# Grouping the P times V matmuls and respacing the weight blocks of a fused attention and two-mixture kernel

## The chip, the cores and the metric

The kernel runs on one core of a Trainium2 chip. The metric is the device time of one execution in microseconds (us), as the median of several runs. The core has five engines with queues of their own: TensorE (PE; its weight loads are shown as PEld), VectorE (DVE), ScalarE (ACT), GpSimd (POOL) and SyncE (SP), which issues nearly all transfers.

## The reference

Attention for 4 batches x 8 heads, 576 positions, head size 64, with a causal mask and a decay bias from a running sum of s; the heads side by side (512 channels) go through a first mixture with a convolution gate, and that through a second mixture.

```python
scores = scale * q @ k.T                       # per head, 576 x 576
bias = -(cum[:, None] - cum[None, :])          # cum = cumsum(max(s, 0))
scores = where(causal, -1e9, scores + minimum(bias, 0))
attn = softmax(scores); out = attn @ v         # "P times V"
x = heads side by side                         # 4 x 576 x 512
h = maximum(x @ w_in, 0)                       # 512 -> 1024
gate = sigmoid(conv3(h, conv_w))
x = (h * gate) @ w_out                         # 1024 -> 512
u = x + (x.T @ U @ V).T
out = u + maximum(u @ w_ch1, 0) @ w_ch2        # 512 -> 2048 -> 512
```

The weights of the mixtures are 64-bit floats and lie in memory as pairs of 32-bit words.

## The kernel before

**A planner sets the order.** Every piece of work is entered with `plan.op(engine, cost, function, reads, writes)`. `Plan.order()` then walks through a model of time: each engine takes, of the entries whose inputs are ready by the model, the one that was entered first. The program that results has one fixed order on each engine; on the chip each instruction waits for its semaphores in that order. The entries' costs shape the order and do nothing else. PSUM banks (8) are handed out by the same walk, with a limit for each class (`CAPS`).

**Attention.** `att_head(h)` enters the work of head h: the transfers for the next head (`prep4` for heads 0 to 7; `prep` and `place` later), the score tiles (`scores`, `scores4`; the products in line 675 and 691, tile sc), maxima on VectorE (line 636), exponentials on ScalarE (line 653, tile P, p for the last 64 rows), the division by the row sum on GpSimd (line 664). For the head before, `transp` turns P's 128 x 128 blocks on PE (line 798, tile pt) in four groups, each of which ScalarE copies to th (line 352). Heads 0 to 7 (`FS`) take q and k in full precision (tile qkF); later heads split them into two parts (tiles t, placed into qkA and qkB).

**P times V.** `av(h, half)` serves a pair of heads. The first half (query positions 0 to 255) needs group 0 of both heads, the second (256 to 575, 320 columns) groups 1, 2 and 3. Each key block j of a group is one entry before the change: two in the first half, five in the second, of 320, 320, 320, 192 and 64 columns. All entries of a half add into one accumulator ps, so they run in their order; the third entry of the second half is the first that needs group 3. An entry holds two matmuls, one for each head of the pair: their 64 columns of V go to columns 0 and 64 of the array (`tile_position`), their outputs to partitions 0 and 64. The profile shows each as two instructions (line 824, tile av). A copy to x follows (line 837), then x's split into xh and xl, on which `m1_in` works.

**First mixture.** `m1_in` multiplies x by the weight blocks w1h and w1l (line 868, tile h) and `m1_out` the gated result by the blocks w1o (line 910, tile y). The parts of batch b are entered among the heads of batch b + 1; PE takes them when attention has nothing ready. They are entered from head 9 on, the first `m1_out` at head 11.

**Weight blocks.** `w1_jobs` are 16 blocks: eight of the first product, then eight of the second. After `att_head(h)`, the loop at the end of the kernel enters each block n with `W1_AT[n] == h`. `load_split` makes a transfer of 512 KB into one of two raw buffers (SP, line 524), a scaling on ScalarE (line 501), three integer operations on VectorE (line 504 once, line 514 twice, tile wf_w), a cast on ScalarE (line 352) and a subtraction on GpSimd (line 364). `load_cw` brings the convolution's 24 columns in the same way at head `CW_AT`. SP issues its transfers in the planned order, and one that waits for a raw buffer holds up those behind it.

**Second mixture.** Behind attention come the splits of u and the weights, the products ma_S and ma_A (line 1153) and the products my (line 1252).

Of the kernel before, what the change touches and what calls it, by code (L numbers as in the profile page):

```python
# [35 lines left out]

WI, WO, WP, WM = 0.3, 1.5, 0.3, 0.2

W1_AT = [0, 1, 1, 2, 3, 4, 5, 5, 6, 7, 7, 8, 9, 10, 10, 11]
CW_AT = 9  # L40
MIX_AT = 12

AHEAD = 80
# [8 lines left out]
def f32(ap):  # L52
    return ap.bitcast(F32)
# [255 lines left out]
def tile_attention_moe_mixer(  # L309
# [21 lines left out]
    def act(n, fn, r, w, extra=0):  # L331
        return plan.op("ACT", (157 if st.get("late") else 53) + n * 0.834 + extra, fn, r, w)

    def pool(n, fn, r, w, two=False, extra=125):
        return plan.op("POOL", ((280 if st.get("late") else 148) + n * 2.1) if two else (37 + n * 0.834 + extra), fn, r, w)
# [8 lines left out]
    def pe(ns, fn, r, w):  # L344
        return plan.op("PE", ns, fn, r, w)
# [5 lines left out]
    def hi_act(out, src, r, w, n):  # L351
        act(n, lambda: nc.scalar.copy(out(), src()), r, w)  # L352
# [10 lines left out]
    def lo_pool(out, src, hi, r, w, n):  # L363
        pool(n, lambda: nc.gpsimd.tensor_tensor(out(), src(), f32(hi()), ALU.subtract), r, w, two=True)  # L364


    st = {}
# [12 lines left out]
    def ring(pool_, cls, count, shape, dtype, name, at={}):  # L380
        n = at[pool_, cls] = at.get((pool_, cls), -1) + 1
        return pool_.buf(f"{cls}{n % count}", shape, dtype, name)

    def bank(cls, name):
        b = Buf(banks, None, [128, 512], F32, name, [banks.opened])
        b.cls = cls
        banks.live.append(b)
        plan.banked.append(b)
        return b
# [93 lines left out]
    for t in p4s:  # L483
        o = pool(64, lambda t=t: nc.gpsimd.memset(t[:, S:640], 0.0), [], [(t, "pad")], extra=0)
# [36 lines left out]
    def load_split(src, h, l, c, n, name):  # L521

        raw = ring(dec, "raw", RINGS["w64"], [128, 512], I64, f"raw_{name}")
        load = dma(n * 1024, lambda: nc.sync.dma_start(out=raw[:, :n], in_=src[:, c : c + n]), [], [raw])
        load.preds.add(st["first"])
        wf = ring(dec, "wf", RINGS["wf"], [128, 512], F32, f"wf_{name}")
        decode64(lambda: wf[:, :n], [wf], raw, n)
        hi_act(lambda: h[:, :n], lambda: wf[:, :n], [wf], [h], n)
        lo_pool(lambda: l[:, :n], lambda: wf[:, :n], lambda: h[:, :n], [wf, h], [l], n)

    def load_cw():
        raw = ring(dec, "raw", RINGS["w64"], [128, 512], I64, "raw_cw")
        dma(24576, lambda: nc.sync.dma_start(out=raw[:, :24], in_=cwU[:, :24]), [], [raw])
        decode64(cw, [cw], raw, 24)
        pool(24, lambda: nc.gpsimd.tensor_scalar(cw(), cw(), 2.0**-8, 1.0, ALU.mult, ALU.mult), [cw], [cw])
# [271 lines left out]
    def av(h, half):  # L807

        b, dt = h // H, h % H // 2
        n, q0, g0 = (256, 0, 0) if half == 0 else (320, 256, 2)  # L810
        vr = st["v", h // 2]
        ps = bank("av", f"av{h}_{half}")
        ops = []
        for g in [0] if half == 0 else [1, 2, 3]:
            for j, i0, i1 in GROUPS[g]:
                ops.append((i0 != g0, g, j, 128 * i0 - q0))
        ops.sort()
        for c, (_, g, j, o) in enumerate(ops):
            w = n - o
            pairs = [st[h + e][f"g{g}"] for e in range(2)]  # L820

            def mms(c=c, j=j, o=o, w=w, pairs=pairs):
                for e, (t, pos) in enumerate(pairs):
                    nc.tensor.matmul(
                        ps[64 * e : 64 * e + 64, o:n],
                        lhsT=vr[:, e, j, :],
                        rhs=t[:, pos[j] : pos[j] + w],
                        start=c == 0,
                        stop=c == len(ops) - 1,
                        tile_position=(0, 64 * e),  # L830
                    )

            pe(max(4 * w / 2.4, 160), mms, [vr, *(t for t, _ in pairs)], [ps])
        if half == 0:
            st["x", b, dt] = ring(ap, "x", RINGS["x"], [128, S], F32, f"x{b}_{dt}")
        x = st["x", b, dt]
        act(n, lambda: nc.scalar.copy(x[:, q0 : q0 + n], ps[:, :n]), [ps], [(x, half)])
        if half == 1:
            th = ring(xp, "xh", RINGS["xs"], [128, S + 2], F32R, f"xh{b}_{dt}")
            tl = ring(xp, "xl", RINGS["xs"], [128, S + 2], F32R, f"xl{b}_{dt}")  # L840
            for t in (th, tl):
                plan.op(
                    "POOL",
                    60,
                    lambda t=t: nc.gpsimd.memset(f32(t[:, 0 : S + 2 : S + 1]), 0.0),
                    [],
                    [(t, "pad")],
                )
            hi_act(lambda: th[:, 1 : S + 1], x, [x], [(th, "x")], S)
            lo_pool(lambda: tl[:, 1 : S + 1], x, lambda: th[:, 1 : S + 1], [x, (th, "x")], [(tl, "x")], S)  # L850
            xs[b, dt] = (th, tl)
# [441 lines left out]
    for c, n in ((0, 384), (512, 224)):  # L1293
        o = pool(n, lambda c=c, n=n: nc.gpsimd.memset(mask[:, c : c + n], 0.0), [], [(mask, c)], extra=0)
# [15 lines left out]
    def att_head(h):  # L1310
# [21 lines left out]
        if h > 0:  # L1332
            transp(h - 1, 1)
            if h % 2 == 0:
                av(h - 2, 0)
# [7 lines left out]
        if h > 0 and h % 2 == 0:  # L1343
            av(h - 2, 1)
# [28 lines left out]
    for h in range(NH + 1):  # L1373
# [11 lines left out]
        for n, (f, c) in enumerate(w1_jobs):  # L1385
            if h == W1_AT[n]:
                load_split(w1[f], w1h[f, c], w1l[f, c], c, 512, f"w1_{f}_{c}")
        if h == CW_AT:
            load_cw()
# [88 lines left out]
    for g in range(2):  # L1478
        blk = (w2a, u1p)[g].buf(f"u{g}", [128, 2 * 7 * S], F32R, f"w2_{g}")
        for i in range(7):  # L1480
            f = 7 * g + i
# [89 lines left out]
```

## Time and profile before

| | us |
|---|---|
| median of 3 runs (lowest to highest) | 837.72 (836.69 to 840.6) |
| the profiled execution | 835.59 |
| span of the profiled execution | 833.8 |
| PE busy in the span | 797.2 |
| DVE busy | 544.3 |
| ACT busy | 453.4 |
| POOL busy | 361.7 |

The profile is one execution; its span runs from the first to the last instruction. Times in a row are from the span's start. Matmuls overlap in PE's pipeline and their drawn lengths hold part of that overlap, so the distance between two starts says more than a length, and PE at full busy share isn't PE at its peak. Lines give the place in the kernel's text, and out<-in the tiles.

### The profile page before, as it was taken

Reading aid. Unit: us, or ns where it says so; the run is one execution under the profiler, and the core shown is the slowest. Engines: PE = TensorE matmul, PEld = TensorE weight load, DVE = VectorE, ACT = ScalarE, POOL = GpSimd, SP = SyncE. Lnnn points to the kernel's source line nnn. Section 1 sums busy time; section 2 is a strip of 40 time slices with the busy share of each in tenths; the row PEclk is TensorE's granted clock in tenths of the full one; section 3 lists DMA queues with packets and bytes.
Section 4 is the critical chain, followed back from the end, with each engine's and each line's share of the span. In section 5 each row is a group of like instructions: output and inputs, shape, how many; then the busy total and the mean of one; then the engine's idle time right before and its main releaser. Section 6 shows DMA issues by size and latency. Waiting matters only on the chain. (4 is left out here: it accounts for less than half of the span.)

```text
span 833.8 us, 15389 instructions
## 1 busy us (share of the span) xinstructions
PE 797.2 (96%) x5300; PEld 706.9 (85%) x5300; DVE 544.3 (65%) x1182; ACT 453.4 (54%) x1144; POOL 361.7 (43%) x441
## 2 busy tenths in 40 slices
PE   4989899999999999999998999999999999999998
PEld 2556687999889998989988998999998888888888
DVE  6878987635855377556898989777689632323232
ACT  4888887758868488676666334334344322222212
POOL 3768574543436344383275866455574200000000
PEclk9999999999999999999999999999999999999999
DMA  7656765644456256030225445546378563635443
GB/s 211 184 156 188 187 162 133 153 112 103 145 132 151 66 121 196 17 108 1 83 84 190 142 132 184 168 143 196 120 220 292 154 199 101 182 108 179 116 127 98
DMA packets 66310, 119.70 MB, mean 144 GB/s; under 512 B 9396, under 2 KB 34868, under 8 KB 66232
## 3 DMA queue, kind: packets, MB, share of 16 engines
q1 hardware_dynamic: 66160, 118.70, 49.1%
q8 instruction: 42, 0.69, 0.4%
q14 instruction: 36, 0.29, 0.1%
q10 hardware_dynamic: 72, 0.01, 0.0%
HBM read 68.81 MB, written 28.90 MB: 117 GB/s over the span
## 5 line engine op out<-in xcount | busy, mean ns | idle before, releaser
L1252 PE MATMUL my<-mh,w 128*128 128x512 f32 (+1 forms) x560 | 158.8, 368 | 0.0
L1153 PE MATMUL ma_S<-u,W 128*128 128x288 f32 x768 | 119.8, 296 | 5.6 <-DVE s L1169 5.5
L1233 DVE SCALAR_TENSOR_TENSOR ml<-ml,mh 128x512 fp32r<-128x512 f32 (+1 forms) x80 | 53.2, 672 | 107.9 <-ACT mh L1230 107.9
L1252 PEld LDWEIGHTS my<-mh,w 128*128 128x128 f32 x560 | 101.6, 189 | 17.5
L1230 ACT ACTIVATE mh<-ml 128x512 fp32r<-128x512 f32 (+1 forms) x80 | 46.8, 589 | 127.9 <-DMA ml<-ch_d 65.8
L1153 PEld LDWEIGHTS ma_S<-u,W 128*128 128x128 f32 x768 | 107.5, 188 | 7.9 <-DVE s L1169 7.9
L664 POOL TENSOR_SCALAR P<-P,sm 128x128 f32<-128x128 f32 (+3 forms) x128 | 75.9, 610 | 86.0 <-DVE sm L727 74.8
L910 PE MATMUL y<-gh,w1o 128*128 128x288 f32 x512 | 112.8, 299 | 0.0
L1252 PE MATMUL my<-ml,w 128*128 128x512 f32 (+1 forms) x280 | 103.0, 368 | 0.0
L636 DVE CUSTOM_DVE_ANT_0 sc<-sc,mask 128x128 f32<-128x128 f32 (+2 forms) x144 | 69.0, 497 | 46.5 <-PE sc L675 37.5
L1153 PE MATMUL ma_A<-u,W 128*128 128x288 f32 x576 | 92.5, 295 | 0.9 <-ACT p L1165 0.9
L364 POOL TENSOR_TENSOR gl<-c,gh 128x288 fp32r<-128x288 f32 x64 | 53.9, 850 | 74.9 <-ACT gh L895 66.8
L910 PEld LDWEIGHTS y<-gh,w1o 128*128 128x128 f32 x512 | 84.9, 188 | 1.5 <-issue 1.0
L868 PE MATMUL h<-xh,w1h 128*128 128x290 f32 x256 | 80.5, 315 | 3.4 <-ACT P L653 1.2
L1153 PEld LDWEIGHTS ma_A<-u,W 128*128 128x128 f32 x576 | 82.0, 188 | 1.6 <-ACT p L1165 1.1
L880 DVE SCALAR_TENSOR_TENSOR c<-h,cw,c 128x288 f32<-128x288 f32 x128 | 64.2, 512 | 24.2 <-ACT c L876 23.4
L868 PE MATMUL h<-xl,w1h 128*128 128x290 f32 x256 | 76.8, 300 | 0.7 <-POOL xl L364 0.7
L868 PE MATMUL h<-xh,w1l 128*128 128x290 f32 x256 | 76.7, 299 | 0.0
L653 ACT ACTIVATE P<-sc,sm 128x128 f32<-128x128 f32 (+3 forms) x128 | 68.2, 537 | 13.0 <-DVE sm L636 10.2
L910 PE MATMUL y<-gl,w1o 128*128 128x288 f32 x256 | 75.1, 293 | 0.0
L352 ACT COPY th<-pt 128x384 f32<-128x384 f32 (+2 forms) x128 | 63.4, 496 | 11.1 <-PE pt L798 9.5
L798 PE MATMUL pt<-ident,P 128*128 128x128 f32 x320 | 60.4, 276 | 1.5 <-POOL P L664 1.5
(139 smaller groups left out, 1748.2 us busy)
## 6 DMA issues: line engine op xcount, KB each, us to landing
ml<-ch_d SPq DMA_DIRECT2D x64, 256.0 KB, 2.8
ch_d<-p SPq DMA_DIRECT2D x64, 144.0 KB, 1.8
raw_w<-w_in SPq DMA_DIRECT2D x16, 512.0 KB, 3.2
raw_w2a<-w_in SPq DMA_DIRECT2D x16, 512.0 KB, 5.3
raw_w2b<-w_in SPq DMA_DIRECT2D x16, 512.0 KB, 4.7
t<-qk_in SPq DMA_DIRECT2D x24, 288.0 KB, 3.0
qkB<-t SPq DMA_DIRECT2D x24, 288.0 KB, 3.7
qkA<-t SPq DMA_DIRECT2D x24, 288.0 KB, 3.9
```

What stands on the lines that cost most here:

```text
L352: act(n, lambda: nc.scalar.copy(out(), src()), r, w)
L364: pool(n, lambda: nc.gpsimd.tensor_tensor(out(), src(), f32(hi()), ALU.subtract), r, w, two=True)
L636: lambda: nc.vector.tensor_tensor_reduce(out=ps[:rows, :w], in0=ps[:rows, :w], in1=mask[:rows, m0 : m0 + w], scale=-0.125, scalar=3.0e38 i ...
L653: lambda: nc.scalar.activation(out(), ps[:rows, :w], ACTF.Exp, bias=low(), scale=-1.0, accum_out=total()),
L664: lambda: nc.gpsimd.tensor_scalar(t[:, :w], t[:, :w], r(), 1.0, ALU.mult, ALU.mult),
L798: nc.tensor.transpose(pt[:, o + rows - 128 : o + rows], d["P"][i][:, 128 * j : 128 * j + 128], turn)
L868: nc.tensor.matmul(ps[:, :W], lhsT=ww, rhs=xx, start=kt + n == 0, stop=kt == KT - 1 and n == 2)
L880: lambda k=k: nc.vector.scalar_tensor_tensor(c(), hh[:, k : k + HS], cw[:, 3 * f + k : 3 * f + k + 1], c(), ALU.mult, ALU.add),
L910: nc.tensor.matmul(ps[:, :HS], lhsT=ww, rhs=xx(), start=f + n == 0, stop=f == NF1 - 1 and n == 2)
L1153: nc.tensor.matmul(ps[:, :HS], lhsT=ww, rhs=uu, start=k == 0, stop=k == 5)
L1233: lambda: nc.vector.scalar_tensor_tensor(ml[:, :n], raw(), 0.0, f32(mh[:, :n]), ALU.max, ALU.subtract),
L1252: nc.tensor.matmul(ys[c][dt][:, :n], lhsT=ww, rhs=xx[:, :n], start=f + k == 0, stop=f == NF2 - 1 and k == 2)
```

## The change

P times V of a half becomes one entry with all its matmuls, in the order that they had; its cost for the planner is 160 plus the time of the columns, where each entry had the time of its columns or 160. The 16 weight blocks stand one at each of heads 0 to 7 (first product), then two at each of heads 8 to 11 (second product); before, heads 1, 5 and 7 had two, and heads 8, 9, 10 and 11 had one, one, two and one. The convolution's columns move from head 9 to head 8.

```diff
-W1_AT = [0, 1, 1, 2, 3, 4, 5, 5, 6, 7, 7, 8, 9, 10, 10, 11]
-CW_AT = 9
+W1_AT = [0, 1, 2, 3, 4, 5, 6, 7, 8, 8, 9, 9, 10, 10, 11, 11]
+CW_AT = 8
...
         ops.sort()
-        for c, (_, g, j, o) in enumerate(ops):
-            w = n - o
-            pairs = [st[h + e][f"g{g}"] for e in range(2)]
-
-            def mms(c=c, j=j, o=o, w=w, pairs=pairs):
-                for e, (t, pos) in enumerate(pairs):
+        ts = {g: [st[h + e][f"g{g}"] for e in range(2)] for _, g, _, _ in ops}
+
+        def mms():
+            for c, (_, g, j, o) in enumerate(ops):
+                w = n - o
+                for e, (t, pos) in enumerate(ts[g]):
                     nc.tensor.matmul(
                         ps[64 * e : 64 * e + 64, o:n],
...
-            pe(max(4 * w / 2.4, 160), mms, [vr, *(t for t, _ in pairs)], [ps])
+        pe(160 + sum(2 * (n - o) / 1.2 for *_, o in ops), mms, [vr, *(t for ps_ in ts.values() for t, _ in ps_)], [ps])
```

## Rows read from the trace of the kernel before

**Rows 1.** Busy time by stretch; the first line names the columns.

```profile
core 0: us, PE busy (x) PEld busy (x) DVE busy (x) ACT busy (x) POOL busy (x), PEclk, DMA share, GB/s
20.00:68.60 48.60, 44.70 (x262) 26.72 (x263) 38.13 (x104) 39.65 (x111) 36.57 (x43) 0.96 0.63 181
68.60:123.00 54.40, 48.51 (x341) 41.12 (x340) 49.42 (x122) 46.60 (x133) 38.42 (x47) 0.97 0.69 178
123.00:361.00 238.00, 237.79 (x1801) 212.46 (x1800) 142.62 (x432) 176.28 (x499) 107.63 (x175) 1.00 0.47 116
...
440.00:640.00 200.00, 191.41 (x1386) 186.56 (x1387) 164.89 (x288) 82.97 (x181) 119.13 (x111) 1.00 0.53 173
```

**Rows 2.** Tiles qkF and qkB: ns min/median/max, first and last start, forms.

```profile
L675 PE MATMUL sc<-qkF x64: 275/486/1061, 8.4 to 67.7; 128*128 128x128 f32 x16, 128*128 128x256 f32 x16, 128*128 128x384 f32 x16, 128*128 128x512 f32 x16
...
L675 PE MATMUL sc<-qkB x32: 222/336/502, 68.6 to 128.3; 128*128 128x288 f32 x6, 128*64 128x288 f32 x6, 128*128 128x128 f32 x5, 128*128 128x256 f32 x5
```

**Rows 3.** PE in order of time, 62.7 to 66.3 us: start, length, operation, count.

```profile
62.71 0.38 PE L798 MATMUL pt<-ident,P 128*128 128x128 f32 x2
63.02 0.76 PE L824 MATMUL av<-th,vr 128*64 128x320 f32 x4
63.71 0.33 PE L798 MATMUL pt<-ident,p 128*128 128x128 f32 x1
63.87 0.38 PE L798 MATMUL pt<-ident,P 128*128 128x128 f32 x2
64.09 0.60 PE L675 MATMUL sc<-qkF 128*128 128x256 f32 x2
64.62 1.74 PE L824 MATMUL av<-th,vr 128*64 128x320 f32 x16
66.28 0.44 PE L798 MATMUL pt<-ident,P 128*128 128x128 f32 x2
```

**Rows 4.** PE in order of time, 357.9 to 360.9 us.

```profile
357.88 0.38 PE L798 MATMUL pt<-ident,P 128*128 128x128 f32 x2
358.19 0.76 PE L824 MATMUL av<-th,vr 128*64 128x320 f32 x4
358.88 0.40 PE L910 MATMUL y<-gh,w1o 128*128 128x288 f32 x1
359.12 0.29 PE L910 MATMUL y<-gl,w1o 128*128 128x288 f32 x1
359.25 0.29 PE L910 MATMUL y<-gh,w1o 128*128 128x288 f32 x1
359.48 1.20 PE L824 MATMUL av<-th,vr 128*64 128x320 f32 x12
360.60 0.40 PE L910 MATMUL y<-gh,w1o 128*128 128x288 f32 x1
```

**Rows 5.** PE in order of time: the first run of av.

```profile
28.15 0.87 PE L824 MATMUL av<-th,vr 128*64 128x256 f32 x8
```

**Rows 6.** PE's waits, 20 to 68.6 us: total us, times, longest.

```profile
PE pt L798 <- POOL p L664: 1.9, 1, 1.9
PE sc L691 <- DMA qkF<-cc: 1.5, 1, 1.5
```

**Rows 7.** PE's waits, 68.6 to 123 us.

```profile
PE pt L798 <- ACT P L653: 1.4, 1, 1.4
...
PE h L868 <- POOL xl L364: 0.7, 1, 0.7
```

**Rows 8.** Groups by line and shape, 0 to 125 us: busy us, mean ns, idle.

```profile
L514 DVE SCALAR_TENSOR_TENSOR wf_w<-raw_w,wf_w 128x512 int32<-128x512 int32 x32 | 28.6, 892 | 0.4
...
L504 DVE TENSOR_SCALAR wf_w<-raw_w 128x512 int32<-128x512 int32 x16 | 9.8, 614 | 3.8 <-ACT raw_w L501 2.5 <-POOL P L664 0.9 <-issue 0.4
```

**Rows 9.** Tile wf_w: ns min/median/max, first and last start.

```profile
L514 DVE SCALAR_TENSOR_TENSOR wf_w<-raw_w,wf_w x32: 660/760/1646, 16.3 to 109.0; 128x512 int32<-128x512 int32 x32
...
L364 POOL TENSOR_TENSOR w1o<-wf_w,w1o x8: 1275/1280/1730, 64.8 to 112.1; 128x512 fp32r<-128x512 f32 x8
```

**Rows 10.** Waits of SP's queue, 10 to 125 us.

```profile
SPq L524 <- DVE wf_w L514: 18.9, 11, 4.4
```

**Rows 11.** Line 910, 90 to 140 us: ns min/median/max, first and last start.

```profile
L910 PEld LDWEIGHTS y<-gh,w1o x32: 187/188/191, 119.9 to 139.1; 128*128 128x128 f32 x32
```

## Prediction

> **What bounds the kernel now.** I read the table of stretches first [rows 1]: the reader is to see where TensorE (PE) has idle time at all. From 123 to 361 us PE is busy for 237.79 of 238.00 us; nothing is waited for there, so the stretch lasts as long as PE's own work, and every nanosecond taken out of PE's stream comes off it. From 20 to 68.6 us PE is idle for 48.60 - 44.70 = 3.90 us, from 68.6 to 123 us for 54.40 - 48.51 = 5.89 us, and the granted clock means are 0.96 and 0.97: parts of both stretches ran at the lower of the two levels. From 440 to 640 us VectorE (DVE) is busy for 164.89 of 200 us and PE idles 8.59 us; that stage starts when attention has ended, so it moves with that end.
>
> Then I put heads to times. The score products of heads 0 to 7 read the tile qkF, those of later heads qkB: the last of the first kind starts at 67.7 us, the first of the second at 68.6 [rows 2]. So 20 to 68.6 us is about heads 1 to 7, and 68.6 to 123 us heads 8 to 11, at 54.4 / 4 = 13.6 us a head.
>
> Third, the order of time on PE around P times V (av). The reader is to watch the start of the group after each av group. Two transposes in a row take 0.22 us (63.87 to 64.09), but the two before av take 0.31 (62.71 to 63.02). The four av instructions last 0.69 (63.02 to 63.71), where 320 columns cost 0.54 inside a long run: the 16 from 64.62 to 66.28 have 896 columns a side in 1.66 us, the 12 from 359.48 to 360.60 have 576 in 1.12, so 320 columns more cost 0.54 us, and what is left in any of these runs, 1.12 - 576 x 0.54 / 320 or 0.69 - 0.54, is 0.15. The first transpose behind takes 0.16 (63.71 to 63.87) instead of 0.11 [rows 3, 4]. **One visit to av thus costs 0.09 + 0.15 + 0.05 = 0.29 us beyond its columns.** Between a transpose and y, the first mixture's second product, it costs 0.09 before, 0.15 in the run, and 0.24 (358.88 to 359.12) instead of 0.13 (359.12 to 359.25) behind: 0.35 us [rows 4].
>
> **P times V.** The computation stays; its instructions become contiguous by half. I counted the runs of av in PE's order of time, the first at 28.15 us, the last at 359.48 [rows 4, 5]: 51 runs for 16 pairs. The first half needs one group of transposes and has 18 runs (16, and two split by another product). The second half has five entries on one accumulator in a fixed order, the third of which needs the last transposed group, so it falls into one, two or three runs: 33. After the change there is one run a half, 32. Nineteen visits go: twelve behind 123 us, seven before.
>
> Behind 123 us PE is all that limits: 12 x 0.32 = 3.8 us off (bounds 12 x 0.29 = 3.5 and 12 x 0.35 = 4.2). Before, 7 x 0.29 = 2.0 us leave a PE that is busy 89 to 92% of the time; between 0 (all turns into idle) and 2.0 I take 1.2, nearer to full, as the busy share is.
>
> The one entry becomes ready when the last group is copied, so the first two column blocks (2 x 0.54 us) move behind that copy, and x with its two splits comes up to 1.08 us later. Where PE has other work this is free; it isn't free for the last pair of the first batch, where PE waits 0.7 us for xl [rows 7]. Between 0 and +1.1 I take +0.5. Queued behind a waiting entry on PE are the next head's scores, for which VectorE and ScalarE wait. PE is handed the entry only when the planner has the last copy done, and the cost the planner has for it (about 2.2 us for the second half) is near the 1.66 us of its last 896 columns plus 0.54, so I add no wait.
>
> **Weight blocks, heads 0 to 7.** A block is one DMA of 512 KB, one ScalarE pass, 0.61 + 2 x 0.89 = 2.40 us of VectorE [rows 8], a ScalarE cast and a GpSimd subtraction. Eleven blocks stand at heads 0 to 7, after the change eight; heads 1, 5 and 7 lose one each. VectorE is busy 38.13 of 48.60 us there [rows 1]; 7.2 us less gives its scores and maxima a free queue. PE's largest waits there are 1.9 us for a normalised p of head 0, which the moved blocks don't precede, and 1.5 us for head 7's rows (qkF from cc) [rows 6]. Those rows queue behind a block that had itself waited for a raw buffer; with one block a head that buffer is free sooner, so I count this wait as gone. Of the 3.90 - 1.5 us left I take a third, as a third of the decode work leaves: 1.5 + 0.9 = 2.4 us off (bounds 0 and 3.9). What is late next is head 0's p, untouched. Weight parts that PE uses as filler arrive up to one head later; no more than four accumulators wait for them, and I cost this at nothing under the same idle time.
>
> **Weight blocks, heads 8 to 11.** Five blocks become eight: 3 x 2.4 = 7.2 us more of VectorE, in a stretch where it is busy 49.42 of 54.40 us and so has 4.98 left [rows 1]. If the backlog drains behind 123 us, where VectorE is busy only 142.62 of 238, it costs 0; if all of it delays a score, 7.2. I take what can't fit: 7.2 - 5.0 = +2.2. The column scale's decode (24 columns) only moves a head earlier, at no cost. The last block's GpSimd pass starts at 112.1 us and takes about 1.3, and y starts at 119.9 [rows 9, 11]: 6.5 us of lead cover the later last blocks; if it were gone, y's first tiles would wait by what is missing, with first-product work to fill.
>
> **Sum.** -3.8 - 1.2 + 0.5 - 2.4 + 2.2 = -4.7 us. The profiled execution took 835.59 us (span 833.8 and 1.8 around it), so 830.9; it lies 2.1 below the median of the runs, 837.72, for which the same -4.7 gives 833.0. Behind 361 us nothing is edited. The planner orders that part again; I cost it at nothing, with about 2 us either way, a quarter of PE's 8.59 idle there.
>
> **Rivals.** *Given back to collisions on VectorE: no change.* The decode's two-input operation takes 0.66 us at best and 1.65 at worst, 0.89 in the mean [rows 8, 9], with GpSimd busy 38.42 of 54.40 us beside it [rows 1]. If the six moved ones run at the worst, they add 6 x (1.65 - 0.89) = 4.5 us, and the sum is -0.2: 837.5 at the median. For it: both engines are fuller here than where the blocks came from in VectorE's case (91% against 78%). Against it: GpSimd is not (71% against 75%). The Trainium skill, page "SBUF — State Buffer", section "Who interferes with whom", says that a VectorE instruction with two SBUF inputs contends with a GpSimd instruction that reads SBUF; by that rule this rival would be the forecast, and the spread of 0.66 to 1.65 us agrees with it without showing the cause.
>
> *The raw buffers hold the queue: slower.* SP issues in order, and each block's DMA waits until an older block is decoded: 18.9 us in eleven waits, the longest 4.4 [rows 10]. Behind it stand the next head's transfers (place, the next pair's q, k and V). Two blocks in a head make 2 x 4.4 us of waits in 13.6 us, and it fits only while decoding doesn't slip. If the three added blocks each hold SP for 4.4 us and PE waits for all of it, 13.2 replaces the 2.2: -3.8 - 1.2 + 0.5 - 2.4 + 13.2 = +6.3, 844.0 at the median. Break-even is at 6.9 us on the path, and over 11.1 it is measurably slower. Against it: PE waits for no such transfer from 68.6 to 123 us now, its largest releasers being ScalarE and GpSimd [rows 7].
>
> *More than forecast.* The early terms give their bounds (-2.0 and -3.9), and backlog and late x cost nothing: -3.8 - 2.0 - 3.9 = -9.7, 828.0 at the median. For it: short stalls under the drawn length of a matmul don't show as idle.
>
> *The visits don't count.* If the 0.29 us were only an artefact of how matmuls are drawn, grouping would give nothing: 0.5 - 2.4 + 2.2 = +0.3, 838.0. Against it: starts are recorded, and the difference repeats beside transposes and beside y.
>
> **How the numbers follow.** 0.5% of 837.72 is 4.2 us, about what a measurement tells from no change. Forecast 0.57 (own range 829 to 836), collisions 0.18, visits that don't count 0.05, slower queue 0.11, more 0.09. The forecast's middle is just over the bound, so 0.41 of its 0.57 are faster, 0.15 the same and 0.01 slower; with "more" faster is 0.50, with both cases of no change the same is 0.38, and slower 0.12. The range leaves out half of "more" and most of the slower case: 827 to 841.
>
> **What would show it.** Right: 32 runs of av; the stretch from about 123 us to the end of attention 3.8 us shorter at 100% PE; no wait for qkF from cc; PE idle from 20 to 68 us under 2 us; VectorE near 95% in heads 8 to 11, PE idle there up by about 2 us. Wrong: extra PE idle in heads 8 to 11 over 7 us, released by qkA or qkB transfers or by VectorE; new gaps after 440 us; or runs of av that save less than 0.29 us each.

## The result and the profile after

The changed kernel takes 831.32 us (median of 4 runs, 830.42 to 831.95) against 837.89 (4 runs, 836.69 to 840.6): a ratio of 0.9916, 95% interval 0.989 to 0.9943, or 6.6 us off. The prediction was 833.0. The two profiles differ by less, 830.2 against 833.8 us of span: the profiled execution of the kernel before was quicker than its timed ones (835.59), that of the kernel after the slowest of its own (831.95).

The page of the changed kernel, its first part (busy us, share of the span, instructions):

```profile
PE 791.6 (95%) x5300; PEld 709.2 (85%) x5300; DVE 538.2 (65%) x1182; ACT 454.3 (55%) x1144; POOL 360.0 (43%) x441
```

PE's busy time fell by 5.6 us. The stretches that answer to [rows 1]:

```profile
core 0: us, PE busy (x) PEld busy (x) DVE busy (x) ACT busy (x) POOL busy (x), PEclk, DMA share, GB/s
20.00:68.60 48.60, 43.03 (x278) 28.12 (x279) 40.40 (x115) 41.96 (x117) 35.85 (x42) 1.00 0.61 169
68.60:123.00 54.40, 47.62 (x339) 41.27 (x338) 44.22 (x110) 46.08 (x127) 37.92 (x47) 0.97 0.72 181
123.00:361.00 238.00, 237.25 (x1809) 215.25 (x1806) 144.87 (x436) 178.74 (x507) 110.68 (x179) 1.00 0.48 120
440.00:640.00 200.00, 194.02 (x1393) 188.56 (x1392) 162.97 (x285) 82.35 (x179) 117.07 (x109) 1.00 0.53 171
```

The reader is to see that PE's busy time in the first stretch is lower than in [rows 1] while it ran more instructions there (278 against 262): fewer visits, and a granted clock of 1.00 against 0.96. Idle time did not shrink: 5.57 us (48.60 - 43.03) and 6.78 us (54.40 - 47.62) in the first two stretches, where it was 3.90 and 5.89. VectorE in the second stretch is at 81%, not fuller. What answers to [rows 2], the last start from qkF and the first from qkB:

```profile
L675 PE MATMUL sc<-qkF x64: 272/486/847, 8.7 to 64.6; 128*128 128x128 f32 x16, 128*128 128x256 f32 x16, 128*128 128x384 f32 x16, 128*128 128x512 f32 x16
...
L675 PE MATMUL sc<-qkB x144: 218/335/505, 65.4 to 345.3; 128*128 128x128 f32 x24, 128*128 128x256 f32 x24, 128*128 128x384 f32 x24, 128*128 128x512 f32 x24
```

Head 8's scores begin 3.2 us earlier. PE's waits from 20 to 68.6 us hold no DMA any more [rows 6], only ScalarE's copies and probabilities, 1.0 us at most:

```profile
PE sc L675 <- ACT th L352: 1.9, 3, 1.0
PE h L868 <- ACT P L653: 0.9, 1, 0.9
```

and those from 68.6 to 123 us [rows 7] have three new names, av itself, y and a product h that waits for VectorE:

```profile
PE pt L798 <- ACT P L653: 2.3, 2, 1.8
PE av L824 <- ACT th L352: 1.1, 1, 1.1
PE y L910 <- POOL w1o L364: 1.0, 1, 1.0
PE h L868 <- ACT th L352: 0.9, 1, 0.9
PE h L868 <- DVE c L889: 0.9, 1, 0.9
```

The last pair's second half, of which [rows 4] hold the last two runs, is one:

```profile
355.51 0.29 PE L910 MATMUL y<-gh,w1o 128*128 128x288 f32 x1
355.73 2.28 PE L824 MATMUL av<-th,vr 128*64 128x320 f32 x20
357.94 0.40 PE L910 MATMUL y<-gh,w1o 128*128 128x288 f32 x1
```

I counted 32 runs of av in PE's order of time. Grouped by shape, only the 320-column instructions, many of which had stood in short runs of their own, are drawn shorter; first the kernel after, then the kernel before (busy us, mean ns):

```profile
L824 PE MATMUL av<-th,vr 128*64 128x320 f32 x192 | 29.4, 441 | 1.7 <-ACT th L352 1.7
```

```profile
L824 PE MATMUL av<-th,vr 128*64 128x320 f32 x192 | 33.1, 450 | 0.0
```

The 256-column instructions took 405 ns in the mean in both.

**Where the time went, by marks.** Two kernels are best compared between places where PE has done the same work. I took the 121st and the 181st transpose (the first of head 8's and of head 12's P; for head 8 that is some 9 to 15 us behind its first scores), the 99th instruction of y, and the first ma_A, all counted in PE's order of time. The later rows hold also the experiments below; "runs" are the runs of av behind the 99th y. e5 and e6 hold added matmuls.

| us | 121st transpose | 181st | 99th y | first ma_A | 99th y to ma_A | runs behind |
|---|---|---|---|---|---|---|
| before | 83.1 | 133.3 | 163.5 | 433.9 | 270.3 | 28 |
| after | 78.1 | 130.5 | 161.1 | 429.5 | 268.4 | 18 |
| before, a second profile | 88.3 | 138.8 | 169.1 | 439.5 | 270.4 | 28 |
| e1 grouping alone | 80.1 | 129.2 | 160.4 | 428.5 | 268.1 | 18 |
| e2 blocks alone | 83.1 | 141.2 | 171.2 | 441.6 | 270.4 | 28 |
| e3 visits alone | 86.6 | 138.3 | 168.8 | 437.1 | 268.3 | 18 |
| e4 three blocks left out | 82.2 | 131.4 | 161.2 | 429.2 | 268.0 | 18 |
| e5 extra visits | 87.5 | 139.1 | 171.5 | 460.8 | 289.3 | 63 |
| e6 the same in one place | 86.3 | 136.7 | 168.4 | 451.1 | 282.7 | 36 |
| e7 replanned | 81.8 | 131.8 | 162.6 | 431.4 | 268.9 | 26 |
| e8 one visit a pair | 77.5 | 134.2 | 164.1 | 429.2 | 265.1 | 9 |
| e9 | 88.6 | 140.9 | 171.3 | 439.7 | 268.3 | 18 |
| e10 | 82.1 | 133.2 | 163.5 | 431.9 | 268.4 | 18 |
| e11 three blocks a head later | 82.8 | 133.5 | 163.9 | 434.4 | 270.5 | 28 |

The reader is to see that the column "99th y to ma_A" goes with the number of runs, to 0.5 us, in all kernels without added matmuls but e7: there PE's idle time in that stretch is 0.2 us where it is 1.1 before. Most of what else tells these kernels apart is in the column "99th y". From first ma_A to the end of the span it is 399.9 us before, 401.5 in the second profile of the same kernel and 400.7 after, so the 0.7 us by which the changed kernel is longer there show nothing.

Up to the 99th y PE has run the same 933 instructions in the kernels of the next table. So its time there parts into busy and idle:

| us, up to the 99th y | runs of av | PE busy | PE idle | at 1.2 GHz |
|---|---|---|---|---|
| before | 23 | 142.7 | 20.8 | 6.8 |
| before, a second profile | 23 | 144.5 | 24.6 | 13.7 |
| after | 14 | 137.6 | 23.5 | 3.4 |
| e1 | 14 | 140.5 | 20.0 | 6.8 |
| e2 | 24 | 147.7 | 23.5 | 17.1 |
| e3 | 14 | 141.9 | 27.0 | 10.2 |

The changed kernel is ahead there by PE's busy time (5.1 us less than in the first profile before), not by its idle time (2.6 us more).

### The profile page after: what moved, and what is told of

Same layout as the page of the kernel before. It is cut to its first block, busy times and chain, and to the rows that moved or that the text cites. A ratio compares the mean times of both kernels' runs of the same rounds, so it can differ in the third digit from the quotient of the medians.

```text
span 830.2 us, 15394 instructions
## 1 busy us (share of the span) xinstructions
PE 791.6 (95%) x5300; PEld 709.2 (85%) x5300; DVE 538.2 (65%) x1182; ACT 454.3 (55%) x1144; POOL 360.0 (43%) x441
## 5 line engine op out<-in xcount | busy, mean ns | idle before, releaser
L636 DVE CUSTOM_DVE_ANT_0 sc<-sc,mask 128x128 f32<-128x128 f32 (+2 forms) x144 | 68.6, 498 | 34.5 <-PE sc L675 32.5
```

Source lines behind the costliest of these rows:

```text
L636: lambda: nc.vector.tensor_tensor_reduce(out=ps[:rows, :w], in0=ps[:rows, :w], in1=mask[:rows, m0 : m0 + w], scale=-0.125, scalar=3.0e38 i ...
```

## The experiments

Each ratio is against runs of the kernel before on the same chip, whose medians were 838.42 us (e1 to e4), 837.46 (e5 to e8) and 839.1 (e9 to e11).

**e1: the grouping alone.** The edit of line 818 on, with `W1_AT` and `CW_AT` as before.

> P times V in one entry a half, the weight blocks and the convolution columns where they were before. By the prediction's steps the grouping alone gives -3.8 - 1.2 + 0.5 = -4.5 us, a ratio to the kernel before of 0.9946. Rival, respacing: most of the measured -6.6 us comes from the weight blocks, and the grouping alone stays within 2 us of before (ratio over 0.9975).

Measured: 832.04 us (6 runs, 829.72 to 833.83), ratio 0.9921, interval 0.9903 to 0.9938. The grouping by itself gives what the whole change gives.

**e2: the weight blocks alone.**

```diff
-W1_AT = [0, 1, 1, 2, 3, 4, 5, 5, 6, 7, 7, 8, 9, 10, 10, 11]
-CW_AT = 9
+W1_AT = [0, 1, 2, 3, 4, 5, 6, 7, 8, 8, 9, 9, 10, 10, 11, 11]
+CW_AT = 8
```

> Only the weight blocks and the convolution columns moved, P times V in its seven entries. By the prediction's steps the relief in heads 1 to 7 and the load in heads 8 to 11 nearly cancel: -2.4 + 2.2 = -0.2 us, ratio 1.000. Rival, respacing: 3 us or more come from here (ratio under 0.9965), with heads 0 to 7 ending some 3 us earlier and nothing of it lost in heads 8 to 11.

Measured: 843.56 us (6 runs), ratio 1.0058, interval 1.0037 to 1.0079: 4.9 us slower. The two profiles part between the 121st transpose, which comes at 83.1 us in both, and the 181st, 7.9 us later than before. The largest wait there, PE in order of time, with what ended its wait in brackets:

```profile
83.65 0.34 PE L675 MATMUL sc<-qkA 128*128 128x384 f32 x1
88.59 0.79 PE L675 MATMUL sc<-qkB 128*128 128x512 f32 x1 [4.60 <-ACT P L653]
```

ScalarE in the same microseconds:

```profile
82.64 0.42 ACT L837 COPY x<-av 128x320 f32<-128x320 f32 x1
86.95 0.67 ACT L501 ACTIVATE raw_w<-raw_w 128x512 f32<-128x512 f32 x1 [3.89 <-DMA raw_w<-w_in]
87.51 0.66 ACT L352 CAST xh<-x 128x576 fp32r<-128x576 f32 x1
88.08 0.36 ACT L653 ACTIVATE P<-sc,sm 128x128 f32<-128x128 f32 x1
```

SP's queue ahead of it:

```profile
79.02 1.82 SPq L524 DMA_DIRECT2D raw_w<-w_in  x2
```

Read from the bottom: two blocks of 512 KB, the 13th and 14th of the sixteen by their order, are sent 1.5 us apart. The first lands some 7.9 us after it was sent (the median of the blocks in the kernel before, up to 125 us, is 3.2 us), its scaling stands at the head of ScalarE's queue for 3.89 us, and the probabilities P behind it, done in 0.4 to 0.6 us each, keep PE from its next score for 4.60 us. Two windows at 1.2 GHz follow, 6.8 us each, from 87.8 us, within the wait, and from 98.1 us; the kernel before has one of 3.4 us in these heads. Up to the 99th y e2 has 5.0 us more of busy PE and 2.7 more of idle than the first profile before, so the lower clock behind the wait may weigh more than the wait itself: by my estimate 10.2 us more at half the clock cost up to 5.1 us. The stall that I priced as SP's queue came through ScalarE's.

**e3: the visits alone.** The planner sees the seven entries and their costs as before; the matmuls of a half are issued together at the place of its last entry. PE's order is that of before but for av.

```diff
-            pe(max(4 * w / 2.4, 160), mms, [vr, *(t for t, _ in pairs)], [ps])
+            todo = [*(todo if c else []), mms]
+
+            def run(todo=todo, last=c == len(ops) - 1):
+                for f in todo if last else []:
+                    f()
+
+            pe(max(4 * w / 2.4, 160), run, [vr, *(t for t, _ in pairs)], [ps])
```

> The planner sees the seven entries of before with their costs, so the order of everything else stays as before; only the matmuls of a half are all issued at the place of its last entry. This is the removal of the 19 visits alone. If a visit costs 0.29 to 0.35 us: 3.8 us less from 123 us to the end of attention and about 1 us less ahead of it, -5 us, ratio 0.994. Rival, order: the visits are worth little, the gain of the change comes from another order of the rest, and this kernel is within 1.5 us of before (ratio over 0.998).

Measured: 836.84 us (12 runs, 832.68 to 840.05), ratio 0.9985, interval 0.9967 to 1.0004, which reaches no change. Behind the 99th y the 10 runs that are gone give 2.1 us; ahead of it the profiled execution (840.0) lies between the kernel before's two profiles. Its PE has a wait there that the first profile of the kernel before lacks:

```profile
19.39 0.38 PE L798 MATMUL pt<-ident,P 128*128 128x128 f32 x2
22.79 1.62 PE L675 MATMUL sc<-qkF 128*128 128x128 f32 x4 [3.02 <-DMA qkF<-cc]
```

**e4: the late load taken away.** The changed kernel without three of the eight blocks at heads 8 to 11: the second product uses blocks 0, 2 and 6 a second time in place of 1, 3 and 7.

```diff
+    for f, f0 in ((1, 0), (3, 2), (7, 6)):
+        for w1x in (w1h, w1l):
+            w1x[f, 512] = w1x[f0, 512]
...
-            if h == W1_AT[n]:
+            if h == W1_AT[n] and n not in (9, 11, 15):
```

> The changed kernel with three of the eight blocks at heads 8 to 11 left out: the second product uses the blocks 0, 2 and 6 twice in place of 1, 3 and 7, and their transfers and decoding are gone, so heads 8 to 11 carry five blocks as before and heads 0 to 7 eight as in the changed kernel. If the load moved there costs 2.2 us on the path, the ratio to the kernel before is 0.9916 - 0.0026 = 0.989; if the backlog drains for nothing, it stays at 0.9916; if blocks on the raw buffers hold the queue, over 4 us are gained (under 0.987).

Measured: 829.94 us (5 runs), ratio 0.9888, interval 0.9872 to 0.9905. Against the changed kernel's 0.9916 that is 0.0028 x 838 = 2.3 us for three blocks taken away; the two intervals overlap, so even the sign isn't settled by it. e1, on the same chip, has all sixteen blocks in their places of before and takes 2.1 us more by the medians. Both comparisons price three blocks that are gone, not three blocks that are moved.

**e5 and e6: the price of a visit.** Both keep e3's order and add the same matmuls of zeros (8 columns, whole array) into av's accumulator. In e5 one stands between each two column blocks of a half, in e6 all of a half stand in one place: the same instructions, 3 visits more in each second half, 48 in all.

```diff
+        def add_zero():
+            nc.tensor.matmul(
+                ps[:, 0:8], lhsT=ident[:, 0:128], rhs=zero[:, 0:8], start=False, stop=False
+            )
...
-                for n, f in enumerate(todo if last else []):
-                    if n:
-                        add_zero()
+                for n, f in enumerate(todo if last else []):
+                    if n == 1:
+                        for _ in todo[1:]:
+                            add_zero()
```

(The removed lines are e5's, the added ones e6's.)

> The order of e3 (seven planner entries, matmuls of a half issued together), with a small full-array matmul (8 columns of zeros, added to the accumulator) between the column blocks of a half: one in each first half, four in each second, 80 in all, so 80 extra visits. If a visit costs about 0.29 us, it is 48 x 0.29 = 14 us longer than e6, which has the same 80 small matmuls in one place of each half. Rival, the visits are worth half of it or less in place: 7 us or less between the two.

> The control for e5: the same 80 small matmuls, all of a half between its first and its second block, so one extra visit a half (32) instead of 80. Against e3: 32 x 0.29 = 9 us and the 80 small matmuls themselves (each some 0.03 to 0.11 us, 2 to 9 us) longer by the theory of the visit's price, so 11 to 18 us; by the rival 5 to 13.

Measured: 865.9 us (ratio 1.0335, 1.0313 to 1.0357) and 852.66 (1.018, 1.016 to 1.0199). The difference of 13.24 us over 48 visits is **0.276 us a visit**; with four runs each it may be 0.21 (lowest of e5 less highest of e6, 10.3 us) to 0.32 (15.4 us). From the 99th y to ma_A, where PE is idle for 1.2 us in either, the two profiles differ by 6.6 us for 27 visits, 0.24 each. One second half in e5, in order of time:

```profile
308.89 0.76 PE L832 MATMUL av<-th,vr 128*64 128x320 f32 x4
309.58 0.39 PE L822 MATMUL av<-zero,ident 128*128 128x8 f32 x2
309.90 0.76 PE L832 MATMUL av<-th,vr 128*64 128x320 f32 x4
...
312.71 0.34 PE L832 MATMUL av<-th,vr 128*64 128x64 f32 x4
312.97 0.40 PE L884 MATMUL h<-xh,w1h 128*128 128x290 f32 x1
```

and one in e6:

```profile
302.03 0.76 PE L832 MATMUL av<-th,vr 128*64 128x320 f32 x4
302.72 1.06 PE L822 MATMUL av<-zero,ident 128*128 128x8 f32 x8
303.71 1.74 PE L832 MATMUL av<-th,vr 128*64 128x320 f32 x16
305.37 0.40 PE L885 MATMUL h<-xh,w1h 128*128 128x290 f32 x1
```

From the first av to the product behind it: 4.08 us against 3.34, 0.25 for each of the three visits.

**e7: another plan, nothing else.** Each of the seven entries costs the planner 50 ns more (`max(4 * w / 2.4, 160) + 50`).

> The kernel before with 50 ns more for each of the seven planner entries of a pair and nothing else: no visit is removed by intent, only the planner's times move, and with them the order. Theory: the gain of grouping alone beyond e3 (some 5 us) is an order that fits better, for which the grouped entry itself is needed (PE takes no block early and scores and transposes move ahead): then this stays within 2 us of before. Rival: any nudge of the planner moves the total by several us and the grouped plan was a lucky draw: then this is off by 3 us or more in either direction.

Measured: 836.04 us (12 runs), ratio 0.9988, interval 0.9974 to 1.0003. A new order by itself moved the median by 1.4 us, which the interval doesn't tell from no change.

**e8: one visit a pair.** The changed kernel with the first half entered where the second one is, both at the end.

```diff
-            if h % 2 == 0:
-                av(h - 2, 0)
...
+            av(h - 2, 0)
```

> The changed kernel with the first half held back to the second, so that a pair has one visit of 28 instructions instead of two (16 visits fewer again). By 0.29 us a visit PE has 4.6 us less, about 3 of them behind 123 us; against that the first half's th tiles and x come some 3 us later. Theory: ratio to before 0.988 to 0.990, better than the changed kernel's 0.9916. Rival: the lateness costs more than the visits give, and it is at or above 0.9916.

Measured: 833.12 us (6 runs), ratio 0.9946, interval 0.9926 to 0.9966: not better than two visits. The first table shows both sides of it: behind the 99th y another 9 runs give 3.3 us, and head 12's first transpose comes 3.7 us later than in the changed kernel.

**e9 and e10: is it the place of the scores?** In the planned order before, a pair's second half stands ahead of the next head's third score tile; grouped, it stands behind two or three of that head's score tiles. My theory was that scores issued earlier feed VectorE and ScalarE earlier. e9 takes e3's order and moves the second half of the first five pairs behind the third score tile and its transposes; e10 takes e1 and puts the wider score tiles of the head behind the half.

```diff
+        if w > 256 and rows == 128 and ("av", h - 3) in st:
+            o.preds.add(st["av", h - 3])
```

(e10's; e9 reorders the planned list.)

> The order of e3 (visits merged, seven planner entries) with one thing changed by hand: in the first five pairs the second half of P times V, with what follows from it, is issued behind the next head's third score tile and the transposes between, where e3 issues it ahead of them. The grouped plan puts them in this order. If that is where the grouped entry gains its further 5 us (scores reach VectorE and ScalarE some 2 us earlier in each of heads 2 to 8), the ratio to before falls from e3's 0.9985 to 0.994 or less. Rival: the order of these few entries is worth nothing and the difference lies elsewhere in the plan: 0.997 to 1.000.

> The opposite of e9: P times V grouped and the weight blocks as before (the kernel of e1), but for the planner the next head's score tiles of 384 and 512 columns depend on the pair's second half, so they stand behind it in PE's order. By the theory of the scores ahead the 5 us are lost again: ratio 0.997 to 1.000. Rival: it stays at e1's 0.992.

Measured: e9 843.03 us (8 runs), ratio 1.0046, interval 1.0027 to 1.0066; e10 836.55 (12 runs), 0.9982, interval 0.996 to 1.0005. e10 loses the gain as the theory wants, but e9 doesn't win it: it is slower than before. The theory in this form is wrong. Neither moves one thing alone. In e10, what is seen where the gain goes is a wait for the next pair's scaled q and k, in order of time:

```profile
88.33 0.33 PE L675 MATMUL sc<-qkB 128*128 128x128 f32 x1 [0.92 <-DMA qkB<-t]
...
89.74 0.30 PE L675 MATMUL sc<-qkA 128*128 128x128 f32 x1 [1.08 <-DMA qkA<-t]
...
96.85 0.37 PE L675 MATMUL sc<-qkA 128*128 128x288 f32 x1 [1.33 <-DMA qkA<-t]
```

In e9 transposes wait for GpSimd's normalised P, from 20 to 125 us in all:

```profile
PE pt L811 <- POOL P L676: 5.1, 5, 2.0
PE sc L687 <- ACT x L858: 2.0, 3, 0.9
```

**e11: e2 with one block at head 8** and three at head 11. By the lists the 10th, 12th and 14th blocks stand one head later.

```diff
-W1_AT = [0, 1, 2, 3, 4, 5, 6, 7, 8, 8, 9, 9, 10, 10, 11, 11]
+W1_AT = [0, 1, 2, 3, 4, 5, 6, 7, 8, 9, 9, 10, 10, 11, 11, 11]
```

> The kernel of e2 (P times V in seven entries, blocks respaced) with one block of the second product at head 8 instead of two, and three at head 11. E2's largest stall is 4.6 us of PE at 84 to 88.6 us, while ScalarE stands 3.9 us at a block's scaling whose transfer hasn't landed, with exponentials queued behind it. If the two blocks and the convolution columns at head 8 cause it, the ratio falls from 1.0058 to about 1.000. Rival: the load on VectorE in heads 8 to 11 causes e2's loss, and it stays over 1.004.

Measured: 836.56 us (12 runs), ratio 0.9977, interval 0.9964 to 0.999. The 4.9 us of e2 are gone, head 12's first transpose starts at 133.5 us instead of 141.2, and ScalarE has no wait for raw_w from 60 to 123 us. The 13th and 14th blocks, which stood together in e2's stall, are now sent at 76.6 and 91.4 us. So e2's loss came from that spacing, not from the load on VectorE, which spends 15.0 us on the blocks from 68.6 to 123 us in e11 and 11.8 in e2; which of the three moved blocks cured it isn't separated, and the second block at head 8 is only one of them.

**The kernel before, profiled again.**

> The kernel before, profiled a second time, since its profiled execution of 835.59 us was among its fastest. All theories expect the same order of instructions and some 838 us; the reader sees in which stretch one execution of the same kernel differs from another: by the order of PE's stages it should be the part ahead of 125 us and the windows at the lower granted clock there.

Measured: 842.73 us, span 840.9, 7.1 us more than the first profile of the same program. PE's waits from 10 to 68.6 us:

```profile
PE sc L675 <- DMA qkF<-cc: 4.1, 1, 4.1
PE sc L691 <- DMA qkF<-cc: 2.5, 1, 2.5
```

The first of them ends at 23.57 us, ahead of the first av. What held these rows is read best in e3's trace, which has the same wait. SP's queue there, in order of time:

```profile
17.26 0.37 SPq L524 DMA_DIRECT2D raw_w<-w_in  x1
19.68 0.51 SPq L576 DMA_DIRECT2D qkF<-qk_in  x1
20.42 0.51 SPq L578 DMA_DIRECT2D qkF<-cc  x1
21.84 0.50 SPq L583 DMA_DIRECT2D qkF<-cc  x1
```

and its waits from 17 to 26 us:

```profile
SPq L576 <- DMA raw_w<-w_in: 2.0, 1, 2.0
SPq L583 <- DMA qkF<-qk_in: 0.9, 1, 0.9
```

In the first profile of the kernel before the three transfers went out at 18.64, 19.21 and 19.84 us. So SP stood behind the landing of a weight block, the last row transfer left 2.0 us later, and PE, waiting from 19.8 us on, got its rows late. After the change SP sends the rows ahead of that block:

```profile
16.97 0.51 SPq L576 DMA_DIRECT2D qkF<-qk_in  x1
18.26 0.50 SPq L583 DMA_DIRECT2D qkF<-cc  x1
19.97 0.38 SPq L524 DMA_DIRECT2D raw_w<-w_in  x1
```

So it is in every trace with the blocks respaced (e2, e4, e8 and e11 too); in every trace with the blocks as before (e1, e3, e5, e6, e7, e9 and e10 too) the block goes first, though only two of those, e3 and this second profile, show the long wait. A lower clock comes with the waits: the granted clock is 0.89 from 20 to 68.6 us in both traces, against 0.96 in [rows 1] and 1.00 after the change; in this second profile its windows at 1.2 GHz begin at 21.7 us (6.8 us long) and 62.6 (3.4), the one within the first of the two waits just listed, the other at the end of the second. The clock doesn't tell the kernels apart, though: e1, which has no such wait, has 0.93 there.

## Why the prediction came out

The time was right, 1.7 us from the median, and the mechanism that it leans on most, a price for each visit, is borne out. The rest of the hit is in part luck: the visits behind 123 us gave less than their term and the part ahead more, and the two block terms cancelled as forecast although the shift of work behind them isn't in the traces. Of the signs that I had named for being right, the 32 runs and the end of the wait for qkF came; 3.8 us off behind 123 us, PE idle under 2 us, VectorE near 95% and 2 us more of PE idle in heads 8 to 11 (it was 0.9) did not. One that I had named for being wrong did come: less than 0.29 us saved for each run.

**The price of a visit: right, a little high.** 0.29 us forecast beside transposes; 0.276 by the medians of e5 and e6 with everything else held equal, 0.24 behind the 99th y. The Trainium skill, page "TensorEngine Tiling (Array Packing)", section "Key Properties", says that changing the tiling mode drains TensorE. The trace agrees with it and doesn't show the drain itself: av goes into two column halves of the array, the zeros, y and the transposes use all of it, and going from one to the other and back costs 0.25 us a visit in the rows of e5 and e6. The rival that the visits don't count is out.

**Twelve visits behind 123 us: mis-sized.** The term was -3.8. Ten of the twelve lie behind the 99th y. Before and e3, whose order differs in av alone, take 270.3 and 268.3 us from there to ma_A: 2.0 us for 10 visits, 0.20 each rather than 0.32. Twelve of that price are -2.4. The 9 that e8 takes away are worth 0.37 each, in another planned order, so the price may depend on the neighbours; two rows [rows 4] beside y stood for all of them. That stage was as full as I had it, 237.25 of 238.00 us.

**Seven early visits and the later x, -1.2 + 0.5: the step that failed.** e1 gives 6.4 us, of which about 2 lie behind the 99th y. So the grouping gives about 4 ahead of it, not 0.7, and more than the 2.0 that I had as the most. One part is the visits: nine go ahead of that mark, and PE's busy time up to it is 2.2 us less in e1 than in the first profile before, at the same 6.8 us of lower clock. That is 0.25 a visit, and none of it was lost to idle time, of which e1 has 0.9 us less. In e3, which has the same 32 runs, it was lost: PE's idle time there is 27.0 us, and the kernel gives 1.3 in all. So the other part is what the plan does to the stage in which PE, ScalarE, GpSimd and SP's transfers wait for each other. A new order as such doesn't do it: e7's gave 1.4, e9's cost 3.9.

What can be seen of that part: neither e1 nor the changed kernel waits once for a transfer between 10 and 125 us, while the seven-entry order waits for qkF's rows by 1.5 us in one profile and 6.6 in another. PE's idle time from 20 to 125 us is 9.8 us in the first profile of the kernel before, 13.4 in its second, 15.4 in e3 and 8.5 in e1, but 12.4 in the changed kernel, so idle time alone doesn't explain the change. In the changed kernel the busy time is 5.1 us less up to the 99th y: some 2.2 for nine visits, up to 1.7 (an estimate: half of 3.4 us) for one window fewer at 1.2 GHz, and the rest isn't explained. It isn't only luck with the clock either. At a mean granted clock of 0.99 two runs of e1 took 833.6 and 833.8 us and three of the kernel before on the same chip 839.0 to 840.5; at 0.994 it is 832.0 against 836.8 to 840.3.

**What stays open** is why e1's plan waits less. Its early rows still stand behind a block in SP's queue; the wait at 19.5 us comes ahead of the first av and differs between two executions of one program, and I have one or two profiles of each kernel and can't count how often it comes. e9 and e10 tried the place of the scores, and don't bear it out.

**Relief at heads 1 to 7, -2.4, and load at heads 8 to 11, +2.2: near as a sum, but the shift of work that both rest on did not take place.** A head in `W1_AT` is a rank in the planner's list, not a time: the blocks run ahead of their heads as raw buffers come free. Of the sixteen, ten had begun their two-input operations ahead of head 8's first score before the change, and ten after it. Busy time on tile wf_w, after and then before (VectorE, ScalarE, GpSimd):

```profile
20.00:68.60 48.60, 20.19 (x25) 5.58 (x9) 13.04 (x10) 1.00 0.61 169
68.60:123.00 54.40, 13.17 (x18) 3.72 (x6) 8.58 (x7) 0.97 0.72 181
```

```profile
20.00:68.60 48.60, 21.57 (x27) 5.64 (x9) 13.63 (x10) 0.96 0.63 181
68.60:123.00 54.40, 14.19 (x17) 3.80 (x6) 8.15 (x6) 0.97 0.69 178
```

The forecast moved 7.2 us of VectorE from the first stretch to the second; it is 1.4 us less in the first and 1.0 us less in the second. So nothing drove VectorE to 95%; it is at 81%, and no backlog on it is seen. The wait for qkF's rows is gone, as I counted, but it is gone in e1 too, where the blocks stand as before, and it is there in e2 (1.8 us) and e11 (2.5 us), where they are respaced, so the blocks by themselves aren't the reason. The marks don't price the two terms: head 8's first transpose comes at 78.1 us after the change and at 80.1 in e1, but at 82.2 in e4, which has the changed kernel's blocks at heads 0 to 7, and two profiles of one kernel differ there by 5.2 us. What is seen of a load is PE waiting 1.0 us for the last w1o block, whose GpSimd pass starts at 121.3 us while y began at 116.3: the cover of 6.5 us that I named was gone. In the relief term a third of 2.40 us is 0.8, not 0.9; that makes the sum -4.6 and changes nothing.

**Together the blocks are worth nothing that the intervals show:** the changed kernel against e1, 0.9916 against 0.9921. My -2.4 + 2.2 said so. But that sum isn't a property of the blocks: in the order of before they cost 4.9 us (e2), or gain 1.9 with three of them a head later (e11). The rival "the raw buffers hold the queue" described a stall that this schedule has in e2, 4.60 us of PE behind a transfer of a block, by way of ScalarE's queue rather than SP's; in the grouped order it doesn't arise.

**Collisions on VectorE: not seen.** The decode's two-input operation, [rows 8, 9], after the change:

```profile
L514 DVE SCALAR_TENSOR_TENSOR wf_w<-raw_w,wf_w x32: 669/750/1674, 15.3 to 119.4; 128x512 int32<-128x512 int32 x32
```

Its mean is 842 ns where it was 892, so no added operations ran at the worst; few had moved at all, so the rival met no fair trial. The Trainium skill, page "SBUF — State Buffer", section "Who interferes with whom", has such an instruction contend with a GpSimd instruction that reads SBUF; the spread of 669 to 1674 ns agrees without showing the cause. The mean was 838 ns behind 68.6 us and 849 from 20 to 68.6.

## What to carry to other kernels

Matmuls that use a column half of the array should be issued in one run: each separate visit between whole-array matmuls cost 0.20 to 0.28 us in this kernel, and in the stage that PE fills this came straight off the time. In a stage where four engines and a transfer queue wait for each other, the planned order decides whether what the edit gives shows in the time (e1) or turns into idle time (e3), and can cost as much as the edit is worth (e9, 3.9 us), so a direct effect has to be measured with the order held fixed, and two edits together rather than as a sum of each. Where a planner sets the order, an entry's place in the program doesn't say when its work runs: that is to be read from a trace before a term is built on it. A transfer of 512 KB whose first consumer sits in an in-order engine's queue can stop everything behind that consumer: two of them sent 1.5 us apart kept PE waiting for 4.60 us.

## What the runs showed of the hardware

- The same program took 835.59 us in one profiled execution and 842.73 in another. Of the 7.1 us between the spans 5.6 came up before 170 us: transfers of small rows left SP 2 to 3 us later, and with each long wait of PE (4.1 and 2.5 us) came a window at 1.2 GHz (6.8 and 3.4 us). The other 1.5 us lie behind the first ma_A. One pair of profiles can't tell a change of 4 us here.
- A change in the width of the weights alone doesn't cost what a visit costs: in e6 score products with weights of 128*64 and of 128*128 follow each other at 0.13 to 0.14 us a step (300.68, 300.81, 300.94, 301.07 us). That leaves the change of column tiling as the likely cause of a visit's cost; no run here changes it alone.
- An 8-column matmul of zeros, two instructions, took 0.25 us in a row of four (0.99 us from 302.72 to the next av at 303.71): about half of the 0.54 us that 320 columns of av cost.
